# Second products of two of three GLU units computed transposed in the last set, their partial sums turned through DRAM

## The chip, the cores and the metric

The kernel runs on one core of one Trainium2 chip, as one program in one launch. Time is the device time of that program in microseconds (us). A profile comes from one execution that the hardware profiler watched; its span runs from the first to the last instruction of the core. The engines are called as in the profile: PE (matrix products, with its weight loads as PEld), DVE, ACT and POOL (elementwise work), SP (here it only issues DMAs).

## What is computed

Attention in chunks of 64 tokens, then a mixture of four experts, then a gated linear unit (GLU), over 2304 tokens of 512 numbers, all in float32. Only the GLU matters here:

```python
def _moe2_ref(x, w_gate, w_val, w_out, rms_g):      # x (2304, 512), w_gate and w_val (512, 1536), w_out (1536, 512)
    rms = np.sqrt(np.mean(x * x, axis=-1, keepdims=True) + 1e-06)
    xn = x / rms * rms_g
    g = xn @ w_gate
    silu = g * (1.0 / (1.0 + np.exp(-g)))
    val = xn @ w_val
    return (silu * val @ w_out).astype(np.float32)
```

## The kernel before

Tokens are cut into three sets of six tiles of 128 (`TPS`), and a set into two halves of three tiles, 384 tokens (`NB`). The experts run over all three sets first, then the GLU over all three. The hidden features of the GLU, 1536, are cut into three units; a unit holds two pairs of 256 (`UF`). So the GLU is nine steps of one form, and the change is in the last three, those of the last set.

A step has two phases on PE. In the first, `hidden` makes gate and value of the unit's features: four calls with seven products each (numbers 0, 5, 4, 6, 1, 2, 3), 28 products of six matmuls of 384 columns. In the second, the product with `w_out` is made in the same way, from seven products (0, 6, 4, 5, 1, 3, 2) of sums of blocks; `parted` holds their left sides as a rounded part (`hh`) and a rest (`hl`), and each product is made in three passes over these parts. Product by product the results are added to partial sums: `u2`, which three blocks of the output share, `c22`, `c11`, `c21` and `c12`, over the units of a set.

Two functions make the second phase. `across` keeps a block of `w_out` in PE and streams the 384 tokens past it: 12 matmuls of 384 columns for a product, the result transposed, features of the output down and tokens across. `second` keeps a tile of 128 tokens in PE and streams 256 columns of `w_out`: 18 matmuls of 256 columns, the result as the output wants it. Its third tile goes to sums of its own (`y1`, `y2`, `y3`). The sets before the last use `across`; `across_end` then turns the sums after the set is done, with 32 x 32 transposes on DVE and DMAs that write blocks of 32 columns to the output, while the next set runs. The last set uses `second` for all its units, and the last unit of it (`last`) writes the output straight from its sums.

All other work is laid between the products by generators that advance with a counted clock (`Chains`): the weights (`weights`), the turned sums of the set before (`across_end`) and what comes with the change. `work.pause(us)` lets a generator wait by that clock, not by the chip's; the order in which the generators record DMAs is the order on the SP queue. The weights lie in DRAM, prepared earlier in the kernel: 28 tiles of 256 KB a unit for gate and value (`wgv`, into the twelve slots of `w1p`, line 325) and seven of 512 KB for `w_out` (`wou`, into the four slots of `w2p`, line 403). A tile is loaded when a slot is free.

Of the kernel before, what the change touches and what calls it, by code (L numbers as in the profile page):

```python
# [8 lines left out]
F32 = mybir.dt.float32  # L9
# [9 lines left out]
P = 128  # L19
CH = 64  # L20
SQ = 32
# [61 lines left out]
class Chains:  # L83
# [6 lines left out]
    def add(self, gen, every=0.0, first=False, busy=None, placed=False):  # L90

        c = [gen, every, self.clock, every if busy is None else busy, placed, None]
        self.chains.insert(0, c) if first else self.chains.append(c)
        return c
# [83 lines left out]
def fused_kernel(ctx, tc, qkv, probs, w12, wglu, gvec, out):  # L178
# [4 lines left out]
    nc = tc.nc  # L183
# [9 lines left out]
    NSET = 3  # L193
    TPB = NTILE // NSET // 2
    TPS = 2 * TPB
    NB = TPB * P
# [4 lines left out]
    dram = ctx.enter_context(tc.tile_pool(name="dram", bufs=1, space=DRAM))  # L201
    sm = ctx.enter_context(tc.tile_pool(name="sm", bufs=6))
    tp = Slots(tc, ctx, "tp", 32, [P, 512], F32)
# [4 lines left out]
    w2p = Slots(tc, ctx, "w2", 4, [P, 2, 512], F32R)  # L208
    r64 = Slots(tc, ctx, "r64", 2, [P, 1024], F32)
    attd = {i: dram.tile([KD, P, P], F32, name=f"att_{i}") for i in range(TPS, NTILE)}  # L210
    xnt = [dram.tile([KD, P, NB], F32, name=f"xnt_{b}") for b in range(2 * NSET)]
    away = set()
    psum = ctx.enter_context(tc.tile_pool(name="psum", bufs=1, space=PSUM))
    banks = Banks(psum, [f"b{n}" for n in range(8)])
    work = Chains()
# [12 lines left out]
    add = lambda eng, o, a, b: eng.tensor_tensor(o, a, b, op=ALU.add)  # L228
# [580 lines left out]
    def catch_up():  # L809
        while later:  # L810
            later.pop(0)()
# [204 lines left out]
    acc = {}  # L1016
# [36 lines left out]
    SUMS = ("u2", "c22", "y1", "c11", "c21", "y2", "c12", "y3")  # L1053

    def second(s, u, fps, end, final, aside):
# [4 lines left out]
        low, high, both = slice(0, w), slice(w, 2 * w), slice(0, 2 * w)  # L1060
# [2 lines left out]
                work.force(c, lambda: c not in work.chains)  # L1063
        summed.clear()
        catch_up()
        if u == 0:
            for n in SUMS:
                acc[n] = tp.get(f"out_{n}")
        ac = {n: acc[n] for n in SUMS}
        big, small, opened = {}, {}, set()  # L1070

# [23 lines left out]
                    hh.put(hi)  # L1095
                    hl.put(lo)

        def take(o, ps, cols=both, first=u == 0):
            if first:
                nc.scalar.copy(ac[o][:, cols], ps[:, cols])  # L1100
            else:
                add(nc.vector, ac[o][:, cols], ps[:, cols], ac[o][:, cols])

        def more(n, *names):
            for fp in fps:
                t = plain_h.pop((fp, *names))
                part(fp, n, t[:, :NB], final and end, nc.vector if final and end and n == 3 else nc.gpsimd)()
                (cp if names == ("s4",) else tp).put(t)
# [13 lines left out]

        last = final and end
        mult(0, 0, 0, 0)
        take("u2", big[0])
        more(1, 1, 0)
        if last:
            more(3, 0, 0)
        mult(6, 6, 0, 1)
        take("c22", big[6])  # L1130
        take("y1", small[0])
        if last:
            more(2, "s4")
        else:
# [61 lines left out]
    def across(s, u, fps, end, aside):  # L1196
# [6 lines left out]
        if u == 0:  # L1203
            for n in SIDES:
                acc[n] = [tp.get(f"out_{n}{d}") for d in range(2)]
        ac, open_banks = {n: acc[n] for n in SIDES}, {}

# [65 lines left out]
        if end:  # L1273
            for n in SIDES:
                acc.pop(n)
            work.add(across_end(s, ac), placed=True)

    SIDES = ("u2", "c22", "c11", "c21", "c12")

    def across_end(s, ac):  # L1280
        yield from work.pause(4)
        for o in ("c21", "c12", "c22"):
            for t, u2 in zip(ac[o], ac["u2"]):
                add(nc.gpsimd, t[:, :NB], t[:, :NB], u2[:, :NB])
                yield from work.pause(1.5)
        tp.put(*ac["u2"])
        for o, b, half in (("c11", 1, 0), ("c21", 0, 0), ("c12", 1, 1), ("c22", 0, 1)):
            for d, t in enumerate(ac[o]):
                while not tp.free():
                    yield  # L1290
                q = tp.get("oq")
                yield {"DVE": 0.6}, 1
                nc.vector.transpose(q[:, :NB], t[:, :NB])
                tp.put(t)
                yield from work.pause(1.5)
                i, col = (s * TPS + b * TPB) * P, (2 * half + d) * P
                for g in range(P // SQ):
                    nc.sync.dma_start(
                        out=out[i:i + NB, col + g * SQ:col + (g + 1) * SQ].rearrange("(j r) c -> r j c", r=SQ),
                        in_=q[g * SQ:(g + 1) * SQ, :NB].rearrange("r (j c) -> r j c", c=SQ),  # L1300
                    )
                    yield from work.pause(1.6)
                    yield
                work.add(leave(q))
# [60 lines left out]
    def leave(t):  # L1365
        yield from work.pause(7)
        tp.put(t)
# [20 lines left out]
    with tc.manual_schedule():  # L1388
# [75 lines left out]
        for kind, s in [(kind, s) for kind in ("moe", "glu") for s in range(NSET)]:  # L1464
            moe = kind == "moe"
            final = not moe and s == NSET - 1
            if moe:
                plan = [(e, [u * UF + k for k in range(UF)]) for e in range(E) for u in range(NF1 // 2 // UF)]
            else:
                plan = [(0, [u * UF + k for k in range(UF)]) for u in range(NF2 // 2 // UF)]  # L1470
            ahead = None
            for k, (e, fps) in enumerate(plan):
                end = k == len(plan) - 1
# [70 lines left out]

                if moe:
                    outer(fps, w2, flush, aside)
                elif s < NSET - 1:
                    across(s, k, fps, end, aside)
                else:
                    second(s, k, fps, end, final, aside)  # L1550
        work.force(None, lambda: not work.chains)
# [59 lines left out]
```

## Time and profile before

| what | value |
|---|---|
| median of 3 runs | 1187.9 us (1187.77 to 1189.01) |
| the profiled execution | 1187.55 us, span 1185.8 us |
| PE busy | 1176.3 us, 99% of the span |
| DVE, ACT, POOL busy | 852.3, 469.9, 729.2 us |
| DMA | 308.73 MB, mean 260 GB/s; the hardware queue's packets 80.0% of 16 engines |

The table gives busy time over the whole span. In the rows further down, L1217 is a matmul of `across`, L1084 one of `second`, L799 one of `hidden`; L325 and L403 are the loads of `wgv` and `wou`, L1298 the writes of turned sums to the output.

### The profile page before, as it was taken

Reading aid. Unit: us, or ns where it says so; the run is one execution under the profiler, and the core shown is the slowest. Engines: PE = TensorE matmul, PEld = TensorE weight load, DVE = VectorE, ACT = ScalarE, POOL = GpSimd, SP = SyncE. Lnnn points to the kernel's source line nnn. Section 1 sums busy time; section 2 is a strip of 40 time slices with the busy share of each in tenths; the row PEclk is TensorE's granted clock in tenths of the full one; section 3 lists DMA queues with packets and bytes.
Section 4 is the critical chain, followed back from the end, with each engine's and each line's share of the span. In section 5 each row is a group of like instructions: output and inputs, shape, how many; then the busy total and the mean of one; then the engine's idle time right before and its main releaser. Section 6 shows DMA issues by size and latency. Waiting matters only on the chain.

```text
span 1185.8 us, 21692 instructions
## 1 busy us (share of the span) xinstructions
PE 1176.3 (99%) x7351; PEld 1098.1 (93%) x7351; DVE 852.3 (72%) x1503; ACT 469.9 (40%) x1077; POOL 729.2 (61%) x783
## 2 busy tenths in 40 slices
PE   8999999999999999999999999999999999999998
PEld 7889999999898888999989999999999999999998
DVE  6965554578875777789878788774688747774767
ACT  5544443334334333443353334344725243243322
POOL 5898666678835254667766867556337645385344
PEclk9999999999999999999999999999999999999999
DMA  8579777684979798867888997856998798787895
GB/s 256 201 283 276 212 257 206 214 286 147 334 245 290 208 294 248 299 242 248 281 280 251 325 325 271 290 175 230 317 291 254 252 318 273 256 292 234 257 305 190
DMA packets 244382, 308.73 MB, mean 260 GB/s; under 512 B 106160, under 2 KB 116912, under 8 KB 244272
## 3 DMA queue, kind: packets, MB, share of 16 engines
q1 hardware_dynamic: 243696, 306.83, 80.0%
q8 instruction: 59, 0.97, 0.3%
q10 hardware_dynamic: 576, 0.52, 0.1%
q14 instruction: 51, 0.42, 0.1%
HBM read 232.30 MB, written 74.97 MB: 259 GB/s over the span
## 4 chain that ended last, share of the span: by engine, by line
PE 96%; DMA 1%; DVE 1%; ACT 1%; POOL 0%; issue 0%; SPq 0%; DVEq 0%; ACTq 0%
PE o L1032 33%; PE c_ps L799 16%; PE a_ps L799 14%; PE d_ps L799 14%; PE x L1217 7%; PE b_ps L799 7%; PE x L1084 2%; PE y L1084 1%; DMA qk_b<-in_qkv 1%; PE pv L616 1%; PE sc L532 1%; ACT sq L1316 0%; DMA r<-in_w 0%; DVE out_c L228 0%; DVE out_y L228 0%
## 5 line engine op out<-in xcount | busy, mean ns | idle before, releaser
L1032 PE MATMUL o<-w,hh 128*128 128x512 f32 x1152 | 356.0, 390 | 0.0
L1032 PEld LDWEIGHTS o<-w,hh 128*128 128x128 f32 x1152 | 215.2, 188 | 43.4
L227 POOL TENSOR_TENSOR w<-r,w 128x512 fp32r<-128x512 f32 (+1 forms) x146 | 169.2, 1168 | 101.7 <-ACT w L388 59.9
L1032 PE MATMUL o<-w,hl 128*128 128x512 f32 x576 | 224.3, 389 | 0.0
L799 PE MATMUL c_ps<-x,w 128*128 128x384 f32 x1080 | 216.2, 337 | 0.8 <-DVE d_ps L228 0.4
L799 PE MATMUL a_ps<-x,w 128*128 128x384 f32 x984 | 197.6, 336 | 0.2
L799 PE MATMUL d_ps<-x,w 128*128 128x384 f32 x984 | 197.6, 336 | 0.0
L799 PEld LDWEIGHTS c_ps<-x,w 128*128 128x128 f32 x1080 | 189.1, 188 | 1.9 <-DVE d_ps L228 0.7
L799 PEld LDWEIGHTS a_ps<-x,w 128*128 128x128 f32 x984 | 172.9, 188 | 3.0 <-ACT p L863 1.0
L799 PEld LDWEIGHTS d_ps<-x,w 128*128 128x128 f32 x984 | 172.9, 188 | 0.4 <-POOL x L227 0.4
L1528 DVE SCALAR_TENSOR_TENSOR acc<-o,pr,acc 128x512 f32<-128x512 f32 x126 | 94.1, 748 | 107.2 <-PE o L1032 107.0
L227 POOL TENSOR_TENSOR hl<-silu,hh 128x384 fp32r<-128x384 f32 x50 | 49.8, 1018 | 131.0 <-ACT hh L941 131.0
L1032 PEld LDWEIGHTS o<-w,hl 128*128 128x128 f32 x576 | 108.1, 188 | 22.5
L227 POOL TENSOR_TENSOR w<-tw,w 128x256 fp32r<-128x256 f32 x136 | 112.5, 837 | 5.2 <-ACT w L262 5.2
L228 POOL TENSOR_TENSOR w<-w,sc 128x512 f32<-128x512 f32 x36 | 49.2, 1366 | 88.6 <-DVE sc L447 83.3
L799 PE MATMUL b_ps<-x,w 128*128 128x384 f32 x492 | 98.6, 336 | 0.0
L227 POOL TENSOR_TENSOR hl<-h_s,hh 128x384 fp32r<-128x384 f32 x70 | 73.8, 1075 | 39.4 <-DVE c_ps L228 18.4
L903 ACT ACTIVATE hh<-d_ps 128x384 fp32r<-128x384 f32 x92 | 45.2, 491 | 130.0 <-DVE d_ps L228 129.9
L863 ACT COPY p<-a_ps 128x384 f32<-128x384 f32 x82 | 39.2, 479 | 144.7 <-PE a_ps L799 144.4
L262 ACT CAST w<-tw 128x256 fp32r<-128x256 f32 x136 | 51.9, 404 | 105.7 <-POOL tw L227 101.7
L228 DVE TENSOR_TENSOR u<-b_ps,p 128x384 f32<-128x384 f32 x82 | 45.5, 555 | 65.8 <-PE b_ps L799 43.8
L799 PEld LDWEIGHTS b_ps<-x,w 128*128 128x128 f32 x492 | 86.5, 188 | 0.0
(152 smaller groups left out, 1888.6 us busy)
## 6 DMA issues: line engine op xcount, KB each, us to landing
w<-wgv SPq DMA_DIRECT2D x252, 256.0 KB, 4.5
w<-w1m SPq DMA_DIRECT2D x224, 256.0 KB, 5.1
r<-in_w SPq DMA_DIRECT2D x128, 256.0 KB, 5.0
w<-wou SPq DMA_DIRECT2D x63, 512.0 KB, 5.9
w1m<-w SPq DMA_DIRECT2D x112, 256.0 KB, 4.2
wgv<-w SPq DMA_DIRECT2D x84, 256.0 KB, 4.9
raw<-in_wglu SPq DMA_DIRECT2D x36, 512.0 KB, 4.5
wou<-w SPq DMA_DIRECT2D x42, 256.0 KB, 4.8
```

The source lines that it names most:

```text
L227: sub = lambda eng, o, a, b: eng.tensor_tensor(o, a, b, op=ALU.subtract)
L228: add = lambda eng, o, a, b: eng.tensor_tensor(o, a, b, op=ALU.add)
L262: nc.scalar.copy(halves(out[n])[:, 0], at[part_of[n]])
L532: nc.tensor.matmul(sc[h2][c * CH:(c + 1) * CH, n:n + CH], q, k, start=True, stop=True)
L616: nc.tensor.matmul(ps[n][lo:lo + CH, o:o + CH], vt[a][row:row + CH, hp, c, :], aT[a][row:row + CH, q:q + CH], start=True, stop=True,)
L799: nc.tensor.matmul(ps[:, :NB], wv[:, wi, k, :], xs[n][:, xi, k, :], start=(first and k == 0 and m == 0), stop=(last and k == KH - 1 and m ...
L863: nc.scalar.copy(p1, v(a))
L903: nc.scalar.activation(hi, src, AF.Relu)
L1032: nc.tensor.matmul(ps, hs[fps[k], b, j][hx][:, r * P:(r + 1) * P], w2[2 * k + j][:, wi], start=((k, j, m) == (0, 0, 0)), stop=((k, j, m) = ...
L1084: nc.tensor.matmul(ps[:, o:o + w], parted[fps[q], n][hx][:, t * P:(t + 1) * P], wv[:, q, wi], start=id(ps) not in opened, stop=(n in (1, 2 ...
L1217: nc.tensor.matmul(ps[:, :NB], wv[:, q, wi, d * P:(d + 1) * P], parted[fps[q], n][hx], start=fresh and (q, m) == (0, 0), stop=(n in (1, 2, ...
L1528: nc.vector.scalar_tensor_tensor(out=acc[i], in0=ps, scalar=pr[:, i, e:e + 1], in1=acc[i], op0=ALU.mult, op1=ALU.add,)
```

## The change

In the last set the first two units go through `across` too, and only the third through `second`. At the end of the second unit, a new generator (`across_turned`) adds `u2` to `c22`, `c21` and `c12` on POOL, and `side_turned` turns each of the eight partial sums by a transpose on DVE, writes it in four DMAs to a DRAM tensor (`side`), and after a pause loads it back in the layout of `second`, as `c22` with a part of `y1`, and so on, two loads for each of four sums. The third unit's `second` then starts its own `u2` and the low half of `y1` with a copy instead of a sum. Before the third unit's second phase the new generators are run to their end. The diff:

```diff
--- before.py
+++ after.py
@@ -208,6 +208,7 @@
     w2p = Slots(tc, ctx, "w2", 4, [P, 2, 512], F32R)
     r64 = Slots(tc, ctx, "r64", 2, [P, 1024], F32)
     attd = {i: dram.tile([KD, P, P], F32, name=f"att_{i}") for i in range(TPS, NTILE)}
+    side = {o: dram.tile([NB, 2 * P], F32, name=f"side_{o}") for o in ("c11", "c21", "c12", "c22")}
     xnt = [dram.tile([KD, P, NB], F32, name=f"xnt_{b}") for b in range(2 * NSET)]
     away = set()
     psum = ctx.enter_context(tc.tile_pool(name="psum", bufs=1, space=PSUM))
@@ -1063,9 +1064,13 @@
                 work.force(c, lambda: c not in work.chains)
         summed.clear()
         catch_up()
-        if u == 0:
-            for n in SUMS:
-                acc[n] = tp.get(f"out_{n}")
+        for c in list(turning):
+            if c in work.chains:
+                work.force(c, lambda: c not in work.chains)
+        for c in turning:
+            if c in work.chains:
+                work.force(c, lambda: c not in work.chains)
+        acc["u2"] = tp.get("out_u2")
         ac = {n: acc[n] for n in SUMS}
         big, small, opened = {}, {}, set()
 
@@ -1095,7 +1100,7 @@
                     hh.put(hi)
                     hl.put(lo)
 
-        def take(o, ps, cols=both, first=u == 0):
+        def take(o, ps, cols=both, first=False):
             if first:
                 nc.scalar.copy(ac[o][:, cols], ps[:, cols])
             else:
@@ -1122,13 +1127,14 @@
 
         last = final and end
         mult(0, 0, 0, 0)
-        take("u2", big[0])
+        take("u2", big[0], first=True)
         more(1, 1, 0)
         if last:
             more(3, 0, 0)
         mult(6, 6, 0, 1)
         take("c22", big[6])
-        take("y1", small[0])
+        take("y1", small[0], low, True)
+        take("y1", small[0], high)
         if last:
             more(2, "s4")
         else:
@@ -1273,9 +1279,54 @@
         if end:
             for n in SIDES:
                 acc.pop(n)
-            work.add(across_end(s, ac), placed=True)
+            if s < NSET - 1:
+                work.add(across_end(s, ac), placed=True)
+            else:
+                turning.append(work.add(across_turned(ac)))
 
     SIDES = ("u2", "c22", "c11", "c21", "c12")
+
+    turning = []
+
+    def across_turned(ac):
+
+        yield from work.pause(2)
+        for o, y, cols in (
+            ("c22", "y1", slice(2 * P, 4 * P)), ("c11", "y2", slice(0, 2 * P)),
+            ("c21", "y2", slice(2 * P, 4 * P)), ("c12", "y3", slice(2 * P, 4 * P)),
+        ):
+            for t, u2 in zip(ac[o], ac["u2"]) if o != "c11" else ():
+                add(nc.gpsimd, t[:, :NB], t[:, :NB], u2[:, :NB])
+                yield from work.pause(1)
+            turning.append(work.add(side_turned(o, ac[o], y, cols)))
+        tp.put(*ac["u2"])
+
+    def side_turned(o, ts, y, cols):
+        for d, t in enumerate(ts):
+            while not tp.free():
+                yield
+            q = tp.get("oq")
+            nc.vector.transpose(q[:, :NB], t[:, :NB])
+            tp.put(t)
+            yield from work.pause(1)
+            for g in range(P // SQ):
+                at = d * P + g * SQ
+                nc.sync.dma_start(
+                    out=side[o][:, at:at + SQ].rearrange("(j r) c -> r j c", r=SQ),
+                    in_=q[g * SQ:(g + 1) * SQ, :NB].rearrange("r (j c) -> r j c", c=SQ),
+                )
+                yield from work.pause(0.5)
+            work.add(leave(q))
+        yield from work.pause(7.5)
+        while tp.free() < 2:
+            yield
+        acc[o] = tp.get(f"out_{o}")
+        if y not in acc:
+            acc[y] = tp.get(f"out_{y}")
+        nc.sync.dma_start(
+            out=acc[o].rearrange("p (t n) -> p t n", t=2), in_=side[o][:2 * P].rearrange("(t p) n -> p t n", p=P)
+        )
+        nc.sync.dma_start(out=acc[y][:, cols], in_=side[o][2 * P:])
 
     def across_end(s, ac):
         yield from work.pause(4)
@@ -1544,8 +1595,8 @@
 
                 if moe:
                     outer(fps, w2, flush, aside)
-                elif s < NSET - 1:
-                    across(s, k, fps, end, aside)
+                elif s < NSET - 1 or not end:
+                    across(s, k, fps, end or final and k == len(plan) - 2, aside)
                 else:
                     second(s, k, fps, end, final, aside)
         work.force(None, lambda: not work.chains)
```

On PE, the first product of the last set's first second phase; `x` and `y` are its results, `w2` the `wou` tile, `hh` and `hl` the hidden parts. What is named first behind the arrow streams, the other stays in PE; `x2` is two matmuls. Before:

```order
L1084 MATMUL x_0_13460<-w2_13284,hh_13224 128x256 x2
L1084 MATMUL x_0_13460<-w2_13284,hl_13225 128x256
L1084 MATMUL x_0_13460<-w2_13284,hh_13224 128x256 x2
L1084 MATMUL x_0_13460<-w2_13284,hl_13225 128x256
L1084 MATMUL y_0_13461<-w2_13284,hh_13224 128x256 x2
L1084 MATMUL y_0_13461<-w2_13284,hl_13225 128x256
```

After:

```order
L1223 MATMUL x_00_13466<-hh_13228,w2_13288 128x384 x2
L1223 MATMUL x_00_13466<-hl_13229,w2_13288 128x384
L1223 MATMUL x_00_13466<-hh_13408,w2_13288 128x384 x2
L1223 MATMUL x_00_13466<-hl_13409,w2_13288 128x384
L1223 MATMUL x_01_13467<-hh_13228,w2_13288 128x384 x2
L1223 MATMUL x_01_13467<-hl_13229,w2_13288 128x384
```

The product had 18 matmuls of 256 columns and has 12 of 384; of both the first nine stand here.

On SP, in the first phase of the last unit, near the end of its loads of `wgv` (`w1_` with the product's number); `oq` is a turned sum, `out_0` the output, `side_` the new DRAM tensors. Before:

```order
L325 DMA w1_6_14392<-wgv_5_1_124 128x512
L325 DMA w1_1_14402<-wgv_5_1_124 128x512
L1298 DMA out_0<-oq_14368 32x12x32
L325 DMA w1_2_14418<-wgv_5_1_124 128x512
L325 DMA w1_3_14429<-wgv_5_1_124 128x512
L1298 DMA out_0<-oq_14368 32x12x32
L403 DMA w2_14441<-wou_2_143 128x1024
L403 DMA w2_14443<-wou_2_143 128x1024
```

After:

```order
L326 DMA w1_0_14306<-wgv_5_1_128 128x512
L1314 DMA side_c22_102<-oq_14239 32x12x32
L1314 DMA side_c11_99<-oq_14241 32x12x32
L1314 DMA side_c21_100<-oq_14277 32x12x32
L326 DMA w1_5_14322<-wgv_5_1_128 128x512
L1314 DMA side_c21_100<-oq_14277 32x12x32
L1314 DMA side_c12_101<-oq_14311 32x12x32
L326 DMA w1_4_14342<-wgv_5_1_128 128x512
L1314 DMA side_c22_102<-oq_14325 32x12x32
L1314 DMA side_c11_99<-oq_14327 32x12x32
```

Before, one write stood among some three loads; now two or three writes of the new tensors stand between one load and the next.

On SP again, from the third or fourth `wou` tile of the last unit to the fifth, with what each one waits for (`DMAHW` is a DMA's landing, on one of eight semaphores in turn, so that each DMA waits for the one eight places ahead; `PE_` is PE's progress). Before:

```order
L403 DMA w2_14473<-wou_2_143 128x1024 [waits DMAHW6_49]
L1298 DMA out_0<-oq_14368 32x12x32 [waits DMAHW7_49]
L403 DMA w2_14643<-wou_2_143 128x1024 [waits DMAHW2_49,DMAHW0_49,PE_49]
L403 DMA w2_14669<-wou_2_143 128x1024 [waits DMAHW3_49,DMAHW1_49,PE_49]
L403 DMA w2_14694<-wou_2_143 128x1024 [waits DMAHW4_49,PE_49]
```

After:

```order
L404 DMA w2_14458<-wou_2_147 128x1024 [waits DMAHW5_49]
L1314 DMA side_c12_101<-oq_14398 32x12x32 [waits DMAHW6_49]
L1349 DMA out_0<-oq_14324 32x12x32 [waits DMAHW7_49]
L1326 DMA out_c22_14524<-side_c22_102 128x2x256 [waits DMAHW0_49,Pool_49]
L1329 DMA out_y1_14525<-side_c22_102 128x256 [waits DMAHW1_49,Pool_49]
L1326 DMA out_c11_14528<-side_c11_99 128x2x256 [waits DMAHW2_49,Pool_49]
L1329 DMA out_y2_14529<-side_c11_99 128x256 [waits DMAHW3_49]
L1326 DMA out_c21_14552<-side_c21_100 128x2x256 [waits DMAHW4_49,Activation_49]
L1329 DMA out_y2_14529<-side_c21_100 128x256 [waits DMAHW5_49]
L1326 DMA out_c12_14582<-side_c12_101 128x2x256 [waits DMAHW6_49]
L1329 DMA out_y3_14583<-side_c12_101 128x256 [waits DMAHW7_49]
L404 DMA w2_14639<-wou_2_147 128x1024 [waits DMAHW0_49,PE_49]
```

The eight loads that bring the sums back now stand between the fourth `wou` load and the fifth.

## Rows read from the trace of the kernel before

**Rows 1.** The page: PE's busy time and the engines' shares of the chain.

```profile
PE 1176.3 (99%) x7351; PEld 1098.1 (93%) x7351; DVE 852.3 (72%) x1503; ACT 469.9 (40%) x1077; POOL 729.2 (61%) x783
...
PE 96%; DMA 1%; DVE 1%; ACT 1%; POOL 0%; issue 0%; SPq 0%; DVEq 0%; ACTq 0%
```

**Rows 2.** Timeline of PE, first rows of phases: start us, us, engine, line, operation.

```profile
946.51 0.51 PE L1217 MATMUL x<-hh,w 128*128 128x384 f32 x2
...
961.10 1.20 PE L799 MATMUL a_ps<-x,w 128*128 128x384 f32 x6
...
990.22 0.51 PE L1217 MATMUL x<-hh,w 128*128 128x384 f32 x2
...
1005.01 0.68 PE L799 MATMUL a_ps<-x,w 128*128 128x384 f32 x3
...
1077.99 0.40 PE L1084 MATMUL x<-w,hh 128*128 128x256 f32 x2
...
1093.11 1.21 PE L799 MATMUL a_ps<-x,w 128*128 128x384 f32 x6
...
1122.23 0.40 PE L1084 MATMUL x<-w,hh 128*128 128x256 f32 x2
...
1137.34 1.20 PE L799 MATMUL a_ps<-x,w 128*128 128x384 f32 x6
```

**Rows 3.** Timeline of SP in the last unit: start us, us, issue, count.

```profile
1147.93 4.48 SPq L325 DMA_DIRECT2D w<-wgv  x5
...
1155.02 1.44 SPq L403 DMA_DIRECT2D w<-wou  x3
```

**Rows 4.** By line: SP's issue ns min/median/max, first and last start, then landing.

```profile
L325 SPq DMA_DIRECT2D w<-wgv x18: 319/320/1182, 1136.8 to 1154.2; - x18
...
DMA to landing us min/median/max: 3.1/3.9/5.5
...
L403 SPq DMA_DIRECT2D w<-wou x4: 430/459/1189, 1155.0 to 1157.0; - x4
...
DMA to landing us min/median/max: 4.9/6.9/9.0
...
L403 SPq DMA_DIRECT2D w<-wou x3: 319/319/319, 1168.8 to 1173.1; - x3
...
DMA to landing us min/median/max: 3.6/4.1/4.5
...
L1298 SPq DMA_DIRECT2D out<-oq x6: 377/422/425, 1139.0 to 1154.5; - x6
...
L1298 SPq DMA_DIRECT2D out<-oq x4: 337/468/494, 1117.3 to 1118.8; - x4
...
DMA to landing us min/median/max: 2.9/3.3/3.5
```

**Rows 5.** By line: transposes, ACT's copy of u2, POOL's sums in across_end.

```profile
L1293 DVE STREAM_TRANSPOSE oq<-out_c x16: 565/567/572, 936.8 to 1150.1; 128x384 f32<-128x384 f32 x16
...
L1100 ACT COPY out_u<-x x1: 578/578/578, 1081.4 to 1081.4; 128x512 f32<-128x512 f32 x1
...
L228 POOL TENSOR_TENSOR out_c<-out_c,out_u 128x384 f32<-128x384 f32 x6 | 6.0, 1022 | 0.0
```

**Rows 6.** Busy time by stretch: PE, PEld, DVE, ACT, POOL, clock, DMA share, GB/s.

```profile
1137.50:1166.50 29.00, 29.00 (x170) 29.00 (x169) 19.46 (x38) 7.99 (x17) 8.98 (x9) 1.00 0.87 281
```

**Rows 7.** Timeline of DVE in the last second phase; in brackets its wait.

```profile
1171.25 1.85 DVE L227 TENSOR_TENSOR p<-silu,p 128x384 fp32r<-128x384 f32 x2 [1.22 <-ACT p L941]
```

**Rows 8.** Timeline of SP where it issues in a row.

```profile
1129.74 1.44 SPq L325 DMA_DIRECT2D w<-wgv  x3
1131.22 0.60 SPq L1298 DMA_DIRECT2D out<-oq  x1
1131.86 1.12 SPq L325 DMA_DIRECT2D w<-wgv  x2
```

**Rows 9.** Busy time by stretch, after PE's last product.

```profile
1182.50:1185.80 3.30, 0.00 (x0) 0.00 (x0) 0.00 (x0) 0.00 (x0) 0.00 (x0) 1.00 0.55 182
```

## Prediction

> **What bounds the kernel now.** I read the page first, then TensorE's timeline, then the waits of the last unit, and last the DMA queue. The page says that PE is busy for 99% of the span and holds 96% of the chain that ended last [rows 1]; all other engines hide behind it. The timeline shows why: in the last set one phase of products follows the other without a gap. The gate and value products of a unit take 28 x 1.04 = 29.12 us, and its second products 15.12 and 15.11 us in the two units that the change touches [rows 2]. So there are only two ways in which this change can move the time: it shortens PE's own work, or it makes PE wait for something that so far came in time. What so far comes in time are weights, all issued by the one SP queue. Its rows [rows 3] show how a load is timed in the last unit. A slot of `w1p` comes free when PE has used a tile, so the loads of the last sixteen tiles go out one per product, as the five from 1147.93 on, and land 3.1 to 5.5 us later, 3.9 in the median [rows 4]. The last of the 28 is issued at 1154.2 and used as the 28th product at 1137.34 + 27 x 1.04 = 1165.42. A load has eleven products, 11.4 us, from issue to use; with 3.9 us for landing, SP may be 7.5 us late before PE notices.
>
> **The change on PE.** Where a second product took 18 matmuls of 256 columns, it takes 12 of 384: the same 4608 columns, fewer instructions. The trace has the new form already, in the sets before: a first unit of a set takes 961.10 - 946.51 = 14.59 us, a second unit 1005.01 - 990.22 = 14.79 us [rows 2]. Against 15.12 and 15.11 that gains 0.53 + 0.32 = **0.85 us**, and nothing else in the change can gain.
>
> **The change on DVE, ACT and POOL.** Added are eight transposes on DVE (0.567 us each, [rows 5]: 4.5 us), six sums on POOL (1.02 us each: 6.1 us), and 384-column sums for 512-column ones. In the last unit's first phase DVE is busy 19.46 of 29.00 us and POOL 8.98 [rows 6], so both have room; cost nothing, unless a pair of transposes stands in front of a sum that PE's next bank needs, at most 2 x 0.57 us once or twice, which I keep as the upper bound. In the last unit `u2` is now copied by ACT (0.58 us, [rows 5]) ahead of the casts for which DVE's two `p` rows wait [rows 7], and DVE in turn has one 512-column sum less and one halved. By the order DVE has a sum or a store waiting for it from there to the end, so the copy may cost up to 0.58 us at the end; I take 0.2 where PE is on time, and nothing where PE is late anyway, which is what follows.
>
> **The change on the SP queue.** This is the term that decides. The 32 writes of the partial sums and the eight loads that bring them back go on the queue that issues every weight. The order shows where: after the load of the 18th tile (`w1_6` of `wgv_5_0`), the last that is on time, there stand 42 DMAs before the first `wou` load of the last unit, where 14 stood before; and between that load and the fifth `wou` load there are 17 instead of 5. How fast can SP issue? When it waits for little, three loads of `wou` took 1.44 us [rows 3], four writes of `oq` started 0.50 us apart between 1117.3 and 1118.8 [rows 4], and six mixed issues stand between 1129.74 and 1132.98 [rows 8]: 0.48, 0.50 and 0.54 us each, whatever their size. I take **0.50 us**. The lowest that the rows allow is 0.34 us, the shortest issue of an `oq` write [rows 4]; the highest that I use is 0.56.
>
> Time is counted from the start of the last unit's first phase (now 1137.34 - 0.85 = 1136.49).
> The 18th tile's load goes out when the sixth product is done, at 6 x 1.04 = 6.24 us.
> The last weight tile is the 39th after it: 6.24 + 19.5 = 25.7 us, landing at 29.6 by 3.9 us; PE wants it at 28.08. It is 1.5 us late.
> The first `wou` tile is the 43rd: 27.7 us, landing at 31.7 (the later `wou` loads of before take 3.6 to 4.5 us, so 4.0; [rows 4]); PE wants it at 29.12. It is **2.6 us late**, and the 1.5 are inside that.
> The next three land some 1.8 us behind one another (before, four landed between 1155.0 + 4.9 and 1157.0 + 9.0, 2.0 apart with a small write between them, [rows 4]), and a second product takes 2.16 us, so they hold.
> The fourth `wou` tile lands near 31.7 + 3 x 1.8 = 37.2. A DMA of this queue waits until the one eight places ahead of it has landed (the order's waits go round eight semaphores), and the sixth of the eight loads of sums stands eight places behind that tile; it goes at 37.2, the two others and the fifth `wou` load by 38.7, and that lands at 42.8. PE has by then done four second products, 31.7 + 8.64 = 40.3 us. It is **2.4 us late** (a tile more or less on the way, 2.0 to 3.0). The sums themselves land before that, so DVE has 2.4 us in which to catch up, and the two last `wou` tiles follow in time.
> Sum: 2.6 + 2.4 - 0.85 = **+4.2 us**. What follows the fifth product is as before (6.48 us of PE, the last sums, and the stores up to the span's end). The profiled execution took 1187.55 us with a span of 1185.8; 4.2 more is 1191.7, and since the median shown is 0.35 above that execution, **1192.1 us**.
> Bounds: with 0.34 us the first `wou` tile lands at 24.9 and the fifth near 33, both in time, -0.85 us in all; the queue begins to cost at 0.44. With 0.56 the first is 5.2 late and the second term 2.8, +7.2 us.
>
> The Trainium skill, in "DMA: Bandwidth & Descriptors" (Specifications), says that runs under 512 bytes do not reach full rate. The writes here have runs of 128 bytes. What the rows show: four writes of 48 KB issued between 1117.34 and 1118.8 land 0.27 us apart ([rows 4]: the first after 3.5 us, the last after 2.9), which is 182 GB/s, while the first phase as a whole moved 281 GB/s with the engines busy for 0.87 of it, so 323 at full [rows 6]. They are slower by the byte, but 32 of them are only 8.6 us of the DMA engines. By the rule alone that, and not SP's issuing, would be the price, and the time would be that of the second rival below.
>
> **Rivals.** *The queue keeps up* (not slower). If issue takes 0.44 us or less, all tiles land in time and only PE's gain is left, perhaps with 0.2 us of DVE at the end: 1187.9 - 0.85 = 1187.1 us. For it: most issues of loads and of `oq` writes are only 0.32 and 0.42 us long [rows 4]. Against it: those stand alone or behind a wait; issues in a row are 0.48 and more apart [rows 3, 8].
> *The DMA engines bind, not the queue.* In the first phase they are busy 0.87 of 29.00 us, so 25.2 us; 8.6 for the writes, 4.9 for reading 1.57 MB back at 323 GB/s and 1.6 for the fifth tile make 40.3 us of work against 29.12 + 8.64 = 37.8 us until it is wanted: 2.5 late, minus 0.85, so 1189.6 us. The queue's sum above is later than this, so it holds only if issue is fast.
> *The clock falls in the new gaps.* Two idle stretches of PE of some 2.5 us each might bring the granted clock from 2.4 to 1.2 GHz, and the three products behind the second would take 6.48 us more: 1198.6. Against it: PE stood still from 1182.50 to 1185.80 with a granted clock of 1.00 [rows 9]. The Trainium skill ("TensorE: Matmul & The Clock Gate", What's actually happening) has the clock halved once the engine has been idle; by that rule the gap would cost this, the trace shows 3.3 us of idleness without it.
>
> **How the numbers follow.** A time within 0.2% (2.4 us) of 1187.9 can't be told from no change here. Chances: the queue late as summed 0.58, the engines binding or the queue half late 0.15, the queue keeping up 0.18, the clock 0.07, another way 0.02. Predicted is the first, 1192.1, its own range 1190.3 to 1195. The first, with the clock and a part of the last, is slower: 0.66. The second and third are no change: 0.32. A gain of over 2.4 us has no source: 0.02. For eight in ten I go down to the kept-up queue, 1187.0, and up to 0.56 us of issue with a little on top, 1196.
>
> **What would show it.** Right: PE waits for DMAs of `wou` ahead of the first and of the fifth second product of the last unit, 2 to 3 us each; the touched units' second phases are 14.6 and 14.8 us long; SP issues without a pause from the first write of the sums to the fifth `wou` load, 0.48 to 0.53 us each. Wrong: SP issues of such writes below 0.44 us apart; a wait of PE for a bank that DVE holds; `wou` loads landing later than 5 us though issued in time (then the engines are the cause); a granted clock under 1.00 in the last 20 us.

## The result, and the profile after

| | before | after |
|---|---|---|
| time, median of 6 runs each | 1188.03 us (1187.58 to 1189.01) | 1198.22 us (1195.45 to 1199.74) |
| ratio, 95% interval | | 1.0084 [1.0073, 1.0094] |
| span of the profiled execution | 1185.8 us | 1196.0 us |

The change makes the kernel 10.2 us slower, both by the medians and by the spans. The forecast was 4.2. Nothing new bounds the kernel by the page; its line on the chain that ended last answers to [rows 1], and only DMA has grown, from 1% to 3%:

```profile
PE 94%; DMA 3%; ACT 1%; SPq 1%; DVE 0%; POOL 0%; issue 0%; ACTq 0%
```

The timeline of PE after the change, its phase starts first (they answer to [rows 2]), then the places of the last unit where it waited; in brackets the idle time and what ended it:

```profile
1078.45 0.51 PE L1223 MATMUL x<-hh,w 128*128 128x384 f32 x2
...
1093.26 0.50 PE L800 MATMUL a_ps<-x,w 128*128 128x384 f32 x2
...
1122.38 0.51 PE L1223 MATMUL x<-hh,w 128*128 128x384 f32 x2
...
1136.96 0.50 PE L800 MATMUL a_ps<-x,w 128*128 128x384 f32 x2
...
1166.98 2.06 PE L800 MATMUL d_ps<-x,w 128*128 128x384 f32 x6 [1.82 <-DMA w<-wgv]
...
1172.20 0.51 PE L1089 MATMUL x<-w,hh 128*128 128x256 f32 x2 [1.11 <-DMA w<-wou]
...
1184.14 1.50 PE L1089 MATMUL x<-w,p 128*128 128x256 f32 x6 [3.06 <-DMA w<-wou]
```

The touched second phases last 14.81 and 14.58 us. The last unit's first phase starts at 1136.96 and would end at 1166.08; its first second product starts at 1172.20, 6.12 us late. Four products of 2.16 us later, at 1180.84, the fifth could start; it starts at 1184.14, 3.30 us late. From there PE needs 8.20 us to its end at 1192.34; before, the same three products took 6.64 (1175.09 to 1181.73), so this is 1.56 more. The clock says why. By stretch: busy time of PE, PEld, DVE, ACT, POOL, then granted clock, DMA share and GB/s:

```profile
1167.20:1170.60 3.40, 3.35 (x11) 2.87 (x11) 1.45 (x3) 0.00 (x0) 0.00 (x0) 0.50 0.93 186
...
1180.80:1184.20 3.40, 0.34 (x4) 0.17 (x2) 3.37 (x8) 0.00 (x0) 0.00 (x0) 1.00 1.05 399
1184.30:1187.70 3.40, 3.40 (x17) 3.40 (x17) 0.84 (x3) 0.00 (x0) 0.00 (x0) 0.50 0.61 224
```

While PE stands still (the middle row) its granted clock is 1.00. It falls to 0.50, so from 2.4 to 1.2 GHz, when PE works again, and stays there for 3.4 us, half of which, 1.7 us, agrees with the 1.56. The first fall, behind the waits for `wgv`, costs little here: the two products that it slows end at 1171.09, and the `wou` tile lands at 1172.15.

So the span's 10.2 us are: start of the phase -0.38, first wait +6.12, second wait +3.30, clock +1.56, and behind PE's end -0.41 (1196.0 - 1192.34 = 3.66 against 1185.8 - 1181.73 = 4.07). The timeline of SP, in the stretch that answers to [rows 3], shows where the tiles were:

```profile
1158.54 0.41 SPq L326 DMA_DIRECT2D w<-wgv  x1
1159.00 1.49 SPq L1314 DMA_DIRECT2D side_c<-oq  x3
1160.58 0.41 SPq L326 DMA_DIRECT2D w<-wgv  x1
1161.10 0.38 SPq L1349 DMA_DIRECT2D out<-oq  x1
1161.52 2.08 SPq L1314 DMA_DIRECT2D side_c<-oq  x4
1163.72 0.41 SPq L326 DMA_DIRECT2D w<-wgv  x1
...
1168.02 0.48 SPq L404 DMA_DIRECT2D w<-wou  x1
...
1178.55 0.47 SPq L1329 DMA_DIRECT2D out_y<-side_c  x1
1179.11 1.41 SPq L404 DMA_DIRECT2D w<-wou  x3
```

Ahead of that stretch stand these rows of SP: the load of the 18th tile, and by line the `wgv` loads from 1137 to 1145 with their landing:

```profile
1144.62 0.32 SPq L326 DMA_DIRECT2D w<-wgv  x1
```

```profile
L326 SPq DMA_DIRECT2D w<-wgv x11: 319/430/1005, 1136.6 to 1144.6; - x11
...
DMA to landing us min/median/max: 4.0/5.0/5.9
```

The writes by line, their issue and below it their landing:

```profile
L1314 SPq DMA_DIRECT2D side_c<-oq x32: 303/463/1176, 1145.7 to 1172.2; - x32
...
DMA to landing us min/median/max: 2.2/2.9/5.9
```

From 1144.62 to 1168.02 SP issues almost without a pause, in the median 0.51 us from one DMA to the next, writes of 48 KB and tiles of 256 KB alike; and what it issues lands soon, after 2.9 us in the median. The first `wou` load goes out at 1168.02 (1155.02 before, [rows 3]), the fifth at 1179.11, right behind the last of the eight reads.

### The profile page after: what moved, and what is told of

It reads as the page before. It is cut to its first block, busy times and chain, and to the rows that moved or that the text cites. A ratio compares the mean times of both kernels' runs of the same rounds, so it can differ in the third digit from the quotient of the medians.

```text
span 1196.0 us, 21608 instructions
## 1 busy us (share of the span) xinstructions
PE 1178.7 (99%) x7267; PEld 1098.7 (92%) x7267; DVE 856.3 (72%) x1514; ACT 471.2 (39%) x1081; POOL 736.0 (62%) x789
## 4 chain that ended last, share of the span: by engine, by line
PE 94%; DMA 3%; ACT 1%; SPq 1%; DVE 0%; POOL 0%; issue 0%; ACTq 0%
PE o L1033 33%; PE c_ps L800 15%; PE a_ps L800 14%; PE d_ps L800 14%; PE x L1223 10%; PE b_ps L800 7%; DMA qk_a<-in_qkv 1%; PE pv L617 1%; DMA w<-wgv 1%; DMA w<-wou 1%; PE sc L533 1%; DMA side_c<-oq 0%; PE x L1089 0%; SPq L1314 0%; ACT sq L1367 0%
## 5 line engine op out<-in xcount | busy, mean ns | idle before, releaser
L1033 PEld LDWEIGHTS o<-w,hl 128*128 128x128 f32 x576 | 108.1, 188 | 22.6
L1223 PE MATMUL x<-hh,w 128*128 128x384 f32 x448 | 113.9, 335 | 0.0
```

The lines of the kernel that those rows point to most:

```text
L1033: nc.tensor.matmul(ps, hs[fps[k], b, j][hx][:, r * P:(r + 1) * P], w2[2 * k + j][:, wi], start=((k, j, m) == (0, 0, 0)), stop=((k, j, m) = ...
L1223: nc.tensor.matmul(ps[:, :NB], wv[:, q, wi, d * P:(d + 1) * P], parted[fps[q], n][hx], start=fresh and (q, m) == (0, 0), stop=(n in (1, 2, ...
```

## The experiments

The theories: **A**, the number of issues on SP's queue is the price. **B**, the 16 DMA engines are, with what they move. **C**, the clock falls behind an idle stretch of PE. The times before are those measured along with each run (1187.64 to 1188.70 us).

| run | time, us | ratio to before, 95% interval |
|---|---|---|
| e1: all 40 on ACT's queue | 1205.77 | [1.0132, 1.0162] |
| e2: the 8 reads on ACT's | 1206.47 | [1.0119, 1.0164] |
| e3: the 32 writes on ACT's | 1206.24 | [1.0134, 1.0164] |
| e4: all 40 on POOL's | 1201.42 | [1.0094, 1.0124] |
| e5: changed, PE kept busy in its second wait | 1196.97 | [1.0062, 1.0088] |
| e6: 16 writes on POOL's | 1192.26 | [1.0021, 1.0045] |
| e7: before + 32 writes of 48 KB | 1195.97 | [1.0051, 1.0077] |
| e8: before + 32 writes of 128 bytes | 1187.87 | [0.9987, 1.0004] |
| e9: before + 32 of 48 KB in long runs | 1193.80 | [1.0036, 1.0066] |
| e10: before + 32 of 384 x 4 bytes | 1198.84 | [1.0083, 1.0113] |
| e11: before + 32 writes + 8 reads | 1197.50 | [1.0072, 1.0105] |
| e12: before + 16 writes of 48 KB | 1188.35 | [0.9989, 1.0008] |

**Other queues, e1 to e4.** The edit replaces the queue on the lines of `side_turned`: the first of the three (the writes) in e1 and e3, the two others (the reads) in e1 and e2, all three in e4, there with `nc.gpsimd`:

```diff
-                nc.sync.dma_start(
+                nc.scalar.dma_start(
                     out=side[o][:, at:at + SQ].rearrange("(j r) c -> r j c", r=SQ),
...
-        nc.sync.dma_start(
+        nc.scalar.dma_start(
             out=acc[o].rearrange("p (t n) -> p t n", t=2), in_=side[o][:2 * P].rearrange("(t p) n -> p t n", p=P)
...
-        nc.sync.dma_start(out=acc[y][:, cols], in_=side[o][2 * P:])
+        nc.scalar.dma_start(out=acc[y][:, cols], in_=side[o][2 * P:])
```

> All 40 transfers of the partial sums (32 writes, 8 reads) are issued by ACT's queue instead of SP's; all else as in the changed kernel. Theory A (SP's queue is late: 43 issues of 0.53 us stand between the 18th tile and the first `wou` tile): SP has its loads alone again, the `wou` tiles are there in time, no fall of the clock, and only TensorE's shorter products are left: 1188.0 - 0.85 = 1187.2 us (1186.8 to 1188). If ACT's 40 issues of 0.5 us (20 us beside 8 busy in 29) hold up its casts, up to 1190. Theory B (the 16 DMA engines are full, 0.96 and 1.02 busy in the two stretches): the same bytes in the same time, so the first `wou` tile is still some us late: 1193 or more.

> Only the 8 reads go to ACT's queue; the 32 writes stay on SP's. Theory A: the first wait for `wou` (some 6 us late in all, with the tiles before it) stays, the second (3.3 us) goes, and with it the second fall of the clock (1.7 us): 1198.2 - 5.0 = 1193.2 us. Theory B: the reads move the same bytes at the same time, the second wait stays: 1198.

> Only the 32 writes go to ACT's queue; the 8 reads stay on SP's between the fourth and the fifth `wou` load. Theory A: the first wait goes; SP is ahead by then, so the second goes too unless a read waits for its last write: 1187.2 to 1189 us. Theory B: as the changed kernel, 1196 to 1198.

> All 40 transfers are issued by POOL's queue. Theory A: SP's loads are in time, 1187.2 us if POOL issues in 0.5 us or so; POOL has 17 of 29 us free, so if an issue costs it 1 us, the 40 take more than that and its `hl` differences and the last sums come late: up to 1195. Theory B: 1193 or more in any case.

All four came out slower than the changed kernel. That is against A everywhere; B's "1193 or more" for e1 and e4 holds by the time, but the rows give another cause. I had not priced what a queue does to the engine that issues on it. In e1 no `wou` tile is waited for any more. The one long wait of PE, in its timeline, is for ACT:

```profile
1171.07 2.29 PE L800 MATMUL a_ps<-x,w 128*128 128x384 f32 x6 [15.20 <-ACT p L864]
```

And ACT, in its own timeline of e1, stood still for DMAs:

```profile
1156.48 0.51 ACT L942 CAST hh<-silu 128x384 fp32r<-128x384 f32 x1 [9.41 <-DMA side_c<-oq]
1170.54 0.48 ACT L864 COPY p<-a_ps 128x384 f32<-128x384 f32 x1 [13.55 <-DMA w<-wou]
```

Each DMA of SP and ACT waits for the one eight places ahead of it among the DMAs of both queues; in e4 POOL's go round eight semaphores of their own. On SP only other DMAs stand behind such a wait, on ACT the casts do. e3 shows the same wait of PE (16.3 us); e2 mixes it with its late writes on SP, and its phase began 2.5 us late besides, so it settles nothing about the second wait. In e4, too, PE waits for ACT alone (8.8 us), and ACT for POOL's `h_s` sums (7.8 us the longest), which stand behind the issues. POOL's rows by line, issue ns min/median/max, and SP's timeline of e4:

```profile
L1314 POOL DMA_DIRECT2D side_c<-oq x32: 616/616/818, 1144.3 to 1167.6; - x32
```

```profile
1155.91 1.04 SPq L404 DMA_DIRECT2D w<-wou  x2
1157.54 1.57 SPq L404 DMA_DIRECT2D w<-wou  x2
```

With the writes off its queue SP has the first `wou` load out at 1155.91, not 1168.02, though POOL sends the same 32 writes in 23 us. The stretch 1160 to 1165 of the changed kernel (first) and of e4 (second), with the packets that the DMA engines moved in it, shows what their busy share is worth:

```profile
1160.00:1165.00 5.00, 4.24 (x24) 3.79 (x23) 2.81 (x6) 1.08 (x3) 1.68 (x3) 1.00 0.92 181
...
DMA packets 3482, 0.91 MB, mean 181 GB/s; under 512 B 3232, under 2 KB 3232, under 8 KB 3482
```

```profile
1160.00:1165.00 5.00, 3.64 (x21) 3.32 (x20) 1.53 (x4) 2.20 (x5) 4.99 (x8) 1.00 1.03 355
...
DMA packets 1213, 1.78 MB, mean 355 GB/s; under 512 B 772, under 2 KB 772, under 8 KB 1213
```

The engines count as 0.92 busy at 181 GB/s and as 1.03 at 355. But they do not move the same: in the first stretch most packets are short ones of the writes, in the second `wou` tiles are landing. So these rows do not decide against B; e9, below, does.

**Half on POOL, e6.**

```diff
-                nc.sync.dma_start(
+                (nc.gpsimd if g % 2 else nc.sync).dma_start(
                     out=side[o][:, at:at + SQ].rearrange("(j r) c -> r j c", r=SQ),
```

> The changed kernel with every second write of a turned tile (16 of 32) on POOL's queue; the other 16 and the 8 reads stay on SP's. Theory A (the price is the number of issues on a queue: 0.54 us each on SP, 0.62 on POOL with its sums behind them): 14 fewer on SP ahead of the first `wou` load, which goes out near 1160 and lands before 1166; POOL spends 9.9 us on issues; 1187.2 to 1189 us, at most 1191 if POOL's `h_s` sums come late. Theory B (the DMA engines bind, the bytes are the same): 1196 or more.

It came to 1192.3, above the range of A and below B's. The two waits of PE are shorter at the first place, not at the second:

```profile
1168.08 0.50 PE L1089 MATMUL x<-w,hh 128*128 128x256 f32 x2 [1.53 <-DMA w<-wou]
...
1180.16 0.95 PE L1089 MATMUL x<-w,p 128*128 128x256 f32 x6 [3.19 <-DMA w<-wou]
```

SP needs 19.1 us for the 30 issues from the 18th tile to the first `wou` load (1144.35 to 1163.45), 0.64 each. That is not the price of an issue: the median step is 0.55, and the profile has SP wait in this stretch, for slots that PE must free and for DVE's turned tiles, its longest two entries being:

```profile
SPq L326 <- PE d_ps L800: 1.6, 3, 0.6
SPq L1314 <- DVE silu L925: 0.9, 2, 0.4
```

Whether POOL's issuing slows SP's besides, no run here shows. The reads still stand ahead of the fifth `wou` load, which goes out at 1173.7 and takes 6.3 us to land.

**Filler for the clock, e5.** Ahead of the fifth second product PE does 24 matmuls into a free bank:

```diff
+            for i in range(24):
+                nc.tensor.matmul(
+                    fill[:, :w], hi[:, :P], hi[:, :w], start=i == 0, stop=i == 23, skip_group_check=True,
+                )
         mult(1, 0, 0, 0)
```

> The changed kernel with 24 matmuls of 256 columns (24 x 0.12 = 2.9 us, into a bank that nothing reads) ahead of the fifth second product of the last unit, where TensorE stood 3.1 us waiting for its `wou` tile; no other engine's order changes. Theory C (the idle stretch is what brings the granted clock down behind it, and the 3.41 us at half speed cost 1.7 us): no fall there, 1198.2 - 1.7 = 1196.5 us (1195.7 to 1197.2). Rival (the fall comes with the load or at random and has nothing to do with the idle stretch): 1198.2 and the granted clock still 0.5 behind 1184.

```profile
1182.55 3.04 PE L1173 MATMUL fill<-p 128*128 128x256 f32 x24
...
1186.45 0.98 PE L1089 MATMUL x<-w,p 128*128 128x256 f32 x6 [0.87 <-DMA w<-wou]
```

```profile
1186.40:1190.00 3.60, 3.55 (x29) 3.55 (x30) 1.55 (x3) 0.00 (x0) 0.00 (x0) 1.00 0.85 311
```

The products behind the filler run at a granted clock of 1.00, and from the fifth product's start to PE's end it takes 6.74 us (1186.45 to 1193.19), not 8.20. So C holds for the fall and its price, in the one execution that was traced. The other traces agree: in the last unit of before, e8 and e12 PE never waits, and its clock is 1.00 to its end. The total, 1196.97, lies in the range of C, 8.4 us over its own before where the changed kernel lost 10.2, but the two intervals overlap; the rows carry this, not the medians. In e5's trace the first fall reaches into the second products: the four ahead of the filler take 10.02 us (1172.53 to 1182.55), not 8.64.

**The queue alone, e7 to e12.** These take the kernel before and add to SP's queue, in the places where the change has its own, DMAs that nothing reads. No other engine's order changes:

```diff
+                nc.sync.dma_start(
+                    out=side[o][:, at:at + SQ].rearrange("(j r) c -> r j c", r=SQ),
+                    in_=xr[g * SQ:(g + 1) * SQ, d, 0, :].rearrange("r (j c) -> r j c", c=SQ),
+                )
```

So it stands in e7; in e8 both sides are cut to one row of 32 elements (`in_=xr[g * SQ:g * SQ + 1, d, 0, :SQ]`).

> The kernel before with 32 additional writes of 48 KB (of a tile that is in place, to DRAM that nothing reads) on SP's queue, at the places in its order where the change has its own; no sums, transposes or reads. Theory A: the first `wou` tile of the last unit is 5 to 6 us late, nothing else: 1193 to 1194.5 us. Theory B: the same time. Theory D (what costs is DVE, ACT or POOL work, or waits of the writes for it): 1188.

> As the kernel with 32 additional writes on SP's queue, but each of 128 bytes in place of 48 KB. Theory A (an issue costs SP 0.5 us whatever it moves): as with 48 KB, less the 1 to 1.5 us that come from slow landings: 1191.5 to 1194.5 us. Theory B (bytes and packets on the DMA engines are what costs): 1188 to 1188.5.

e7 loses 7.4 us with no sums, transposes or reads, so theory D falls: the change's work on DVE, ACT and POOL is not needed for a loss of this size. It is above the range of A, which said "nothing else" than the late tile. In e7's trace the unit's first phase starts at 1137.96, so the first second product is due 29.12 us later, at 1167.08; it starts at 1171.92, 4.84 us late. The unit itself starts 0.6 us later than before, and the rest is the clock: the first fall lasts longer here than in the changed kernel and reaches into the second products, which together take 1.62 us more than before:

```profile
1172.00:1175.40 3.40, 3.40 (x16) 3.40 (x17) 0.72 (x2) 2.58 (x6) 2.29 (x4) 0.50 1.09 348
```

e8, to my surprise, loses nothing. That would be B's result, had SP issued at the same pace; it did not. The writes' rows by line in e7 and e8:

```profile
L1294 SPq DMA_DIRECT2D side_c<-xr x32: 358/472/602, 1146.4 to 1172.8; - x32
```

```profile
L1294 SPq DMA_DIRECT2D side_c<-xr x32: 214/250/323, 1146.5 to 1165.9; - x32
```

A tiny write takes SP 0.25 us, not 0.47, so 32 of them fit. Is it bytes (A3) or pieces (A2) that make the difference? The output of e9 is 32 whole rows of 1536 bytes, that of e10 the first 4 bytes of each of the 384 pieces (the inputs likewise):

```diff
-                    out=side[o][:, at:at + SQ].rearrange("(j r) c -> r j c", r=SQ),
+                    out=side[o].rearrange("a c -> (a c)").rearrange("(x r y) -> x r y", r=SQ, x=8)[4 * d + g],
```

```diff
-                    out=side[o][:, at:at + SQ].rearrange("(j r) c -> r j c", r=SQ),
+                    out=side[o][:, at:at + SQ].rearrange("(j r) c -> r j c", r=SQ)[:, :, :1],
```

> As the kernel before with 32 additional writes of 48 KB on SP's queue at the same places, but each laid out as 32 runs of 1536 bytes, not 384 of 128. Theory A2 (what an issue costs SP grows with the pieces of the transfer: 0.25 to 0.3 us for one piece, 0.5 for 384): issues 0.3 to 0.35 us apart, all loads in time, 1187.5 to 1188.8 us. Theory A3 (it grows with the bytes): 0.5 us apart as before, 1194 to 1196.

> The same 32 writes with 384 pieces of 4 bytes each, 1.5 KB in place of 48 KB. Theory A2 (pieces): issues 0.5 us apart and the first `wou` tile late as with the full writes, 1194 to 1196 us. Theory A3 (bytes): as with the tiny writes, 1187.5 to 1188.8.

Neither alone. e9, with a twelfth of the pieces, loses 6.2 us; e10, with a thirty-second of the bytes, 11.2. Their rows by line, e10's landing below its issue:

```profile
L1294 SPq DMA_DIRECT2D side_c<-xr x32: 302/421/482, 1147.1 to 1171.1; - x32
```

```profile
L1294 SPq DMA_DIRECT2D side_c<-xr x32: 302/467/1409, 1146.2 to 1176.8; - x32
...
DMA to landing us min/median/max: 3.5/5.0/6.4
```

From 1.5 KB to 48 KB and from 32 pieces to 384 such a write takes SP 0.42 to 0.47 us in the median, and the next follows some 0.05 to 0.1 us later; the 256 KB loads between them take 0.37 to 0.41. Only the transfer of a single row is cheaper; what in its shape makes it so stays open. e10's further loss fits its slow landing (5.0 us in the median, 2.8 in e7): the wait for the DMA eight places ahead then holds SP too. This was not tried apart. What decides against B is the stretch in which SP falls behind, in e7 (first row) and e9 (second):

```profile
1160.00:1165.00 5.00, 5.00 (x30) 4.85 (x28) 3.49 (x7) 1.49 (x4) 2.03 (x2) 1.00 0.92 183
...
1160.00:1165.00 5.00, 5.00 (x31) 5.00 (x30) 3.52 (x7) 1.86 (x4) 2.03 (x2) 1.00 0.61 155
```

With long runs the engines are busy 0.61 of the time instead of 0.92, yet the last 42 steps of SP up to the first `wou` load still take 21.3 us (1145.84 to 1167.11; 22.6 in e7, 1145.44 to 1168.02), and most of the loss stays: 6.2 against 7.4 us, with overlapping intervals. Engines that are idle for over a third of that stretch do not hold the queue up in it.

Last, e11 adds the reads to e7, and e12 leaves out every second write of e7:

```diff
+        yield from work.pause(7.5)
+        while tp.free() < 2:
+            yield
+        ts = [tp.get(f"back_{o}{n}") for n in range(2)]
+        nc.sync.dma_start(
+            out=ts[0].rearrange("p (t n) -> p t n", t=2), in_=side[o][:2 * P].rearrange("(t p) n -> p t n", p=P)
+        )
+        nc.sync.dma_start(out=ts[1][:, :2 * P], in_=side[o][2 * P:])
+        tp.put(*ts)
```

```diff
+                if g % 2:
+                    yield from work.pause(0.5)
+                    continue
                 nc.sync.dma_start(
```

> The kernel before with the 32 additional 48 KB writes and also 8 reads of what they wrote (into tiles that nothing reads) on SP's queue, between the fourth and the fifth `wou` load of the last unit, where the change has them; no sums, no transposes, no turned products. Theory A: the second wait of 3 us and its fall of the clock (1.7 us) come on top of the 32 writes' cost: 1196.0 + 3 to 5, so 1199 to 1201 us, which is the changed kernel plus the 0.85 us that its products gain. Rival E (the second wait comes from DVE, ACT or POOL work that the change adds, not from the queue): 1196.

> The kernel before with 16 of the 32 additional 48 KB writes (every second one). Theory A (a queue with room for so many issues; each takes 0.5 us whatever it moves): 28 DMAs stand between the 18th tile and the first `wou` load, which goes out near 6.4 + 29 x 0.52 = 21.5 us after the start of the phase and lands at 25.5, 3.6 us before it is wanted: no cost, 1187.4 to 1188.5 us, where 32 cost 7.4. Rival F (each write costs its share, by the engines' time): half of 7.4, so 1191 to 1192.

In e12 half the writes cost nothing that the runs can tell from zero, where all of them cost 7.4 us. So the price is not a share for each write (F); there is room for so many, and only what exceeds it costs. Engines with idle time to fill would have such room too, so this row by itself does not tell the queue from them. Its `wou` loads, in SP's timeline, go out at 1160.20, 5.2 us later than before, and still in time:

```profile
1160.20 2.08 SPq L404 DMA_DIRECT2D w<-wou  x3
```

e11, with the reads, loses 9.9 us, 2.5 more than e7 where I expected 3 to 5 (by medians that each scatter over 3 us); that lies between the forecasts of A and E. Its fifth tile is late as in the changed kernel: SP's timeline has the last read at 1178.55 and the `wou` loads behind it, to the tenth of a microsecond where the change has them:

```profile
1178.55 0.42 SPq L1306 DMA_DIRECT2D back_c<-side_c  x1
1179.06 2.49 SPq L404 DMA_DIRECT2D w<-wou  x3
```

PE's wait for its fifth product, which starts at 1185.15, is put down to DVE (1.79 us). But the tile's load takes 6.0 us to land, up to 1185.0, so PE could not have started more than 0.1 us earlier; how long it would wait for DVE with the tile in time was not tried. The wait is shorter than the 3.3 us of the changed kernel because PE comes later: behind the first wait the clock is down for 6.8 us, and the four products take 11.35 us, not 8.64. Behind the second wait it does not fall here:

```profile
1170.80:1177.60 6.80, 5.59 (x26) 5.59 (x27) 2.71 (x5) 3.09 (x7) 6.72 (x7) 0.50 1.09 346
...
1177.70:1191.80 14.10, 12.31 (x102) 11.99 (x100) 9.41 (x18) 0.00 (x0) 1.02 (x1) 1.00 0.80 271
```

So 40 DMAs on SP's queue, with nothing else of the change, lose 9.9 us; less the 0.85 that the products gain that would be 9.0 of the 10.2 measured. The 1.2 between lie within the scatter of the runs. The terms are the same, a late first tile, a late fifth tile and a slowed clock, but not each of the same size.

No version here beats the kernel before. The most that one could win is the 0.85 us, 0.07%, which these runs could not tell from none.

## Why the prediction was wrong

The mechanism of the late queue was right, its size was not, and the clock, which the sum held at nothing, fell: 4.2 us forecast, 10.2 measured, and the range ended at 1196. By its own steps:

- **PE's gain of 0.85 us: right.** 14.81 and 14.58 us, 29.39 together, against 29.38 forecast, though the longer one is the first of the two and not the second; why, no run shows. That the last unit starts only 0.38 us earlier has another cause: one wait of 0.42 us for `wgv` at 973.12, in a unit that the change does not touch.
- **DVE, ACT and POOL: right.** PE waits for none of them anywhere in the last unit. The copy of `u2` costs nothing, since PE is late.
- **The first `wou` tile, 2.6 us late: the step that failed most.** It is 6.1. *"The 18th tile's load goes out when the sixth product is done, at 6 x 1.04 = 6.24 us"* failed: it goes out at 1144.62, so at 7.66. The loads of that stretch take 5.0 us in the median to land, SP runs into the wait for the DMA eight places ahead, and I had applied that rule only at the second wait. That is 1.4 us, of which 0.4 stood already in the kernel before: there the same load went out at 1144.0, 6.7 us after the start of its phase. *"I take 0.50 us"* was right for the step in the middle (0.51) and wrong for the row: 43 steps in the 23.4 us from 1144.62 to 1168.02 are 0.544 each, which adds 1.9 us over that many. The sum had no pauses, and the row has some, the longest an issue of 1.18 us; what held that one the trace does not show. The tile lands 4.2 us after its issue, where 4.0 was taken.
- **The fifth `wou` tile, 2.4 us late: 3.3.** The order was as forecast, eight reads and then the load; it is used 5.0 us after its issue, where 4.1 was taken. The load waited for the landing of the fourth tile, by way of the sixth read, as the prediction says.
- **The clock, dismissed with a chance of 7 in 100: it fell, at 1.6 us, not 6.48.** I held [rows 9] against it: 3.3 us of idleness at 1.00. But PE's clock also shows 1.00 in the idle stretch of 1180.80 to 1184.20 here; the fall stands behind it, in the work, and behind the end of before there is no work in which it could cost anything. There it falls too, behind the stretch of the row and 5.2 us after PE's end:

```profile
1186.90:1187.70 0.80, 0.00 (x0) 0.00 (x0) 0.00 (x0) 0.00 (x0) 0.00 (x0) 0.50 0.00 0
```

The row said nothing on the question. The price was wrong as well, since the clock is back after 3.4 us and not at the end of three products. That this rival's time, 1198.6, lies near the measured 1198.2 is luck: its 6.48 us stand in place of three misses of other terms. On the idle engine's halved clock the Trainium skill ("TensorE: Matmul & The Clock Gate", What's actually happening) was right and my reading of the row wrong: e5 has no fall behind the second wait, where the engine was kept busy.
- **Short runs of 128 bytes, weighed by the Trainium skill ("DMA: Bandwidth & Descriptors", Specifications):** that the DMA engines' time for them would be the price is not borne out. Runs of 1536 bytes cost 6.2 us where runs of 128 cost 7.4, with overlapping intervals. That short runs are slow by the byte agrees with the traces (a share of 0.92 at 183 GB/s in e7, of 0.61 at 155 in e9).
- **The bounds.** The price of an issue, 0.544 us, lay inside its own (0.34 to 0.56). But I let only that one term vary; the start of the row of issues, the second landing and the clock were held at their likeliest. The misses of the first tile, the fifth tile and the clock add to 3.5 + 0.9 + 1.6, and with the 0.5 by which the last unit started later than forecast, less 0.4 at the end, they are, but for rounding, the 6.0 us that the sum was short.

## What to carry to other kernels

Price a DMA first by its place on a queue: count the issues between a load's earliest start and its use, at the spacing that a row of issues shows, its pauses included (0.54 us here), and compare with the room; up to the room it costs nothing (16 writes), and what exceeds it is paid (32 writes). Whether a queue or the engines bind was read here from a queue that issues almost without gaps and whose DMAs land soon (2.9 us in the median), and from a trial that relieved the engines alone (e9); the busy share by itself did not tell. Moving DMAs to a compute engine's queue puts their waits, or on POOL their issuing, in front of that engine's work. Where a wait of PE is forecast, give a lowered clock behind it a term of its own: it cost 1.6 us behind the second wait of the change, 1.6 in e7 and 2.7 in e11 behind the first.

## What was not expected of the hardware

- A write's issue on SP costs much the same for 1.5 KB and 48 KB, in 32 pieces or 384: 0.42 to 0.47 us in a row, and 0.25 us for a single row of 128 bytes. On POOL a write's issue takes 0.62 us of the engine itself.
- The DMA engines show a share of 0.92 at 181 GB/s, where most packets are under 512 bytes, and of 1.03 at 355 GB/s with tiles of 512 KB under way.
- In the changed kernel the granted clock is 1.00 throughout PE's longest idle stretch and 0.50 for the 3.4 us after it. In e7 and e11 it stays at 0.50 for 6.8 us behind the first waits.
